# Two unused 96-byte tiles at the two ends of the SBUF partition, in a one-core fp32 attention and mixer block

## The chip, the core and the metric

The kernel runs on one core of one Trainium2 chip. TensorE (PE in the profile, its weight loads PEld) multiplies matrices, VectorE (DVE) and ScalarE (ACT) work on elements, GpSimd (POOL) does small jobs, and SyncE (SP) issues all transfers. The metric is the device time of one execution in microseconds. Operands of TensorE come from SBUF, 128 partitions wide; a matmul needs one operand that is loaded first (the weights, 128 columns here) and one that is streamed (the moving operand, 128 to 512 columns here). Results go to PSUM.

## The reference

For x of 2048 tokens by 576 columns, with xn the layernorm of x, the output is the sum of three things:

```python
q, k, v = split(xn @ wqkv)                       # 32 heads of 18
o = softmax(q . k[t - 2w], w = 0..7) @ v[t - 2w] # causal window of 8, dilation 2
A = o @ wo
h  = gelu(layernorm(xn) @ w1)                    # 576 x 576
hs = shift(h, [+1, -1, +2, -2] by column quarter) @ w2
x1 = xn + hs
B  = x1 + gelu(layernorm(x1) @ w3) @ w4          # 576 x 4608 x 576
out = x + A + B
```

All of it is fp32. The kernel reaches that accuracy on TensorE by splitting each operand into a rounded part (hi) and the remainder (lo), both as fp32r, and adding hi x hi, hi x lo and lo x hi.

## The kernel before, in words

The work on TensorE comes in stages, all written out in the order in which they run; nothing is planned at run time.

1. **QKV projection** (0 to about 196 us, lines L230 in `q_cg` and L133 in `mm_tok`). For each tile of 128 tokens the normalized tokens, transposed into `xt` by TensorE (L102, L105 in `transposes`; the identity is the moving operand), are the weights, and 288 or 432 columns of `WQ` move. Results are spilled to DRAM through the staging tile `stg`.
2. **First mixer matrix** (about 196 to 264 us, L380 and L395). Slices of `W1` are the weights, 512 tokens of `xt` move; the gelu goes into the eight `h` tiles.
3. **Second mixer matrix** (about 264 to 328 us, L133 again). Slices of the `h` tiles, shifted by one or two floats, are the weights; 288 columns of `W2` move.
4. **The MLP** (about 328 to 1250 us). `up` (L616) takes `W3` as weights and moves 512 columns of `xt` or `x1n`, 14 matmuls for one result. `down` (L636) takes slices of 128 columns of `hi` and `lo` as weights and moves 288 columns of `W4`; 12 matmuls make one result of 128 tokens, 48 make a block of 512. The attention on VectorE runs in between, in slices that a generator hands out (`bg`).
5. **The output projection** (about 1250 to 1318 us, L133 and L764): slices of `oT` as weights, 288 columns of `Wo` moving; then the rows of `Y` are stored.

SBUF is given out by pools that work as two stacks. Pools on the left grow upward from byte 40,608 of the partition, behind the fixed tiles of the pool `base`; pools with `side="right"` grow downward from byte 229,344. A pool that is closed gives its place to the next one on its side. Every tile begins at a multiple of 32 bytes. Tiles that matter to the change, with the byte at which they begin in the partition and that byte modulo 128:

| Tile | Side | Before | mod 128 | After | mod 128 |
|---|---|---|---|---|---|
| Y, ident (pool base) | left | 1152, 38016 | 0, 0 | the same | 0, 0 |
| WQ, W2 | left | 40608 | 32 | 40704 | 0 |
| h00 to h03 | left | 63648, 71872, 80096, 88320 | 32, 64, 96, 0 | each + 96 | 0, 32, 64, 96 |
| hi, lo | left | 45216 to 63648 | 32 | each + 96 | 0 |
| q, k, v, prod, o, L (attention) | left | 67744 and up | 32 (v 96) | each + 96 | 0 (v 64) |
| Wo, oT | left | 65696, 101536 and on | 32 | each + 96 | 0 |
| xin, first raw buffer | left | 109728, 116640 | 32 | each + 96 | 0 |
| second raw buffer, stg | left | 125280, 137952 and on | 96 | each + 96 | 64 |
| xt | right | 192480, 210912 | 96 | each - 96 | 0 |
| W1, W1R, z | right | 165344, 185824, 188384 | 96 | each - 96 | 0 |
| W3, W4, rawf | right | 163296, 178656, 153568 and on | 96 | each - 96 | 0 |
| x1n2, x1n3 | right | 116704, 135136 | 96 | each - 96 | 0 |

The slices that the matmuls take lie at multiples of 128 bytes from the start of their tile, but for three kinds: the 432-column slices of WQ (1728 bytes, so every second one is 64 further on), the slices of `h` (shifted by 4 or 8 bytes, behind two floats of margin) and T4 (8 bytes).

The lines of the prediction's steps:

```python
pe.matmul(ps[:, h, :n], xs(a), ws(b, h), ...)                                  # L133: weights, then moving
pe.matmul(ps, W3[f][:, w, :], x1n[b][:, a, :], ...)                            # L616
pe.matmul(ps[:, k, :HF], h[:, col], w[:, p, k * HF:(k + 1) * HF], ...)         # L636
```

Of the kernel before, what the change touches and what calls it, by code (L numbers as in the profile page):

```python
# [8 lines left out]
F32 = mybir.dt.float32  # L9
# [36 lines left out]
def fused_block(ctx, tc, x, wqkv, wo, w1, w2, w3, w4, out):  # L46
# [4 lines left out]

    ctx.enter_context(tc.manual_schedule())
    base = ctx.enter_context(tc.tile_pool(name="base", bufs=1))
    ring = ctx.enter_context(tc.tile_pool(name="ring", bufs=2, side="right", reuse_waits="tile"))
    psa = ctx.enter_context(tc.tile_pool(name="psa", bufs=2, space=PSUM))
    psb = ctx.enter_context(tc.tile_pool(name="psb", bufs=3, space=PSUM))
    dram = ctx.enter_context(tc.tile_pool(name="dram", bufs=1, space=DRAM))
# [738 lines left out]
```

## Time and profile before

| | |
|---|---|
| Median of 3 runs | 1322.92 us (1322.52 to 1323.04) |
| Profiled execution | 1322.94 us, span 1321.2 us |
| TensorE busy | 1312.1 us, 99% of the span |
| VectorE busy | 921.9 us, 70% |
| ScalarE busy | 348.2 us, 26% |
| Transfers | 93.76 MB, 23.9% of the 16 engines' time |

The page of the profile gives busy times by engine, slices of the span, the DMA queues, the chain of work that ended last, and the costliest groups of instructions. A row of a group reads: line, engine, operation, output tile <- input tiles, shapes, count | busy us, mean ns of one | idle us of the engine just before them, and what ended it. The time of one matmul in such a row is longer than the step from one matmul to the next, since matmuls overlap; the step is read from the chain, whose pieces are given as start, length, engine, tile, line and count. All groups of `W1`, `W2`, `W3` and `W4` stand under the name `W`.

### The profile page before, as it was taken

Reading aid. Unit: us, or ns where it says so; the run is one execution under the profiler, and the core shown is the slowest. Engines: PE = TensorE matmul, PEld = TensorE weight load, DVE = VectorE, ACT = ScalarE, POOL = GpSimd, SP = SyncE. Lnnn points to the kernel's source line nnn. Section 1 sums busy time; section 2 is a strip of 40 time slices with the busy share of each in tenths; the row PEclk is TensorE's granted clock in tenths of the full one; section 3 lists DMA queues with packets and bytes.
Section 4 is the critical chain, followed back from the end, with each engine's and each line's share of the span. In section 5 each row is a group of like instructions: output and inputs, shape, how many; then the busy total and the mean of one; then the engine's idle time right before and its main releaser. Section 6 shows DMA issues by size and latency. Waiting matters only on the chain.

```text
span 1321.2 us, 18855 instructions
## 1 busy us (share of the span) xinstructions
PE 1312.1 (99%) x7894; PEld 1208.0 (91%) x7894; DVE 921.9 (70%) x1332; ACT 348.2 (26%) x633; POOL 35.2 (3%) x92
## 2 busy tenths in 40 slices
PE   8999999999999999999999999999999999999998
PEld 8999998899899999999999999999999999999998
DVE  6443326687676778878868868878877886884454
ACT  4322225411423222222122222223213223122111
POOL 2010100011000000000000000000000000000000
PEclk9999999999999999999999999999999999999999
DMA  7644322020112021221221220220320200212164
GB/s 211 152 107 108 98 68 69 18 82 28 59 30 80 20 71 39 71 71 39 71 71 29 80 71 20 90 71 20 90 71 19 82 28 20 71 42 95 46 192 140
DMA packets 120325, 93.76 MB, mean 71 GB/s; under 512 B 73504, under 2 KB 100000, under 8 KB 120240
## 3 DMA queue, kind: packets, MB, share of 16 engines
q1 hardware_dynamic: 120240, 92.56, 23.9%
q8 instruction: 62, 1.02, 0.3%
q14 instruction: 23, 0.19, 0.0%
HBM read 67.83 MB, written 23.66 MB: 69 GB/s over the span
## 4 chain that ended last, share of the span: by engine, by line
PE 96%; DVE 2%; ACT 1%; SPq 1%; issue 1%; DMA 0%; POOL 0%; DVEq 0%; ACTq 0%; POOLq 0%
PE ps L636 34%; PE p L616 34%; PE ps L133 18%; PE ps L230 3%; PE p L380 3%; PE ps L102 2%; PE p L272 0%; PE p L395 0%; PE p L764 0%; DVE bn L88 0%; PE ps L105 0%; ACT xt L107 0%; DVE xt L111 0%; SPq L370 0%; DVE xt L114 0%
## 5 line engine op out<-in xcount | busy, mean ns | idle before, releaser
L636 PE MATMUL ps<-W,hi 128*128 128x288 f32 x2304 | 397.9, 294 | 0.5 <-DVE oT L114 0.5
L636 PEld LDWEIGHTS ps<-W,hi 128*128 128x128 f32 x2304 | 339.5, 188 | 6.1 <-PE ps L102 0.7
L620 ACT ACTIVATE hi<-p 128x512 fp32r<-128x512 f32 x144 | 86.2, 599 | 619.3 <-PE p L616 619.3
L636 PE MATMUL ps<-W,lo 128*128 128x288 f32 x1152 | 245.3, 294 | 0.0
L616 PE MATMUL p<-xt,W 128*128 128x512 f32 x1008 | 235.4, 390 | 0.0
L616 PE MATMUL p<-x1n,W 128*128 128x512 f32 x1008 | 234.9, 389 | 0.0
L622 DVE TENSOR_TENSOR lo<-g,hi 128x512 fp32r<-128x512 f32 x144 | 99.7, 692 | 193.2 <-ACT g L621 193.2
L639 DVE TENSOR_TENSOR Y<-ps,Y 128x576 f32<-128x576 f32 x288 | 212.8, 751 | 16.3 <-PE ps L636 16.1
L616 PEld LDWEIGHTS p<-x1n,W 128*128 128x128 f32 x1008 | 187.2, 188 | 36.8
L616 PEld LDWEIGHTS p<-xt,W 128*128 128x128 f32 x1008 | 187.1, 188 | 36.9
L636 PEld LDWEIGHTS ps<-W,lo 128*128 128x128 f32 x1152 | 185.4, 187 | 0.0
L133 PE MATMUL ps<-WQ,xt 128*128 128x432 f32 x672 | 135.3, 360 | 0.0
L133 PEld LDWEIGHTS ps<-WQ,xt 128*128 128x128 f32 x672 | 125.2, 188 | 5.2
L111 DVE TENSOR_TENSOR xt<-ps,xt 128x512 fp32r<-128x512 f32 x40 | 27.6, 689 | 87.2 <-ACT xt L110 52.1
L568 DVE TENSOR_TENSOR prod<-q,k 128x1152 f32<-128x1152 f32 x64 | 86.5, 1351 | 0.0
L571 DVE TENSOR_REDUCE L<-prod 128x64 f32<-128x1152 f32 x64 | 86.2, 1347 | 0.0
L621 ACT ACTIVATE g<-p 128x512 f32<-128x512 f32 x144 | 85.4, 593 | 0.0
L548 DVE TENSOR_TENSOR prod<-v,L 128x1152 f32<-128x1152 f32 x56 | 75.6, 1350 | 0.0
L552 DVE TENSOR_TENSOR o<-o,prod 128x1152 f32<-128x1152 f32 x56 | 75.6, 1350 | 0.0
L118 ACT CAST W<-rawf 128x640 fp32r<-128x640 f32 x72 | 50.5, 702 | 68.9 <-PE ps L636 62.2
L133 PE MATMUL ps<-Wo,oT 128*128 128x288 f32 x420 | 59.1, 298 | 0.2
L133 PEld LDWEIGHTS ps<-Wo,oT 128*128 128x128 f32 x420 | 56.2, 188 | 1.4 <-issue 1.4
(103 smaller groups left out, 941.9 us busy)
## 6 DMA issues: line engine op xcount, KB each, us to landing
qkvd<-stg SPq DMA_DIRECT2D x24, 432.0 KB, 3.4
rawf<-in_B_w_dram SPq DMA_DIRECT2D x36, 288.0 KB, 3.0
rawf<-in_B_w_dram SPq DMA_DIRECT2D x36, 256.0 KB, 2.9
xin<-in_A_x_dram SPq DMA_DIRECT2D x16, 288.0 KB, 3.8
q<-qkvd SPq DMA_DIRECT2D x8, 576.0 KB, 3.8
k<-qkvd SPq DMA_DIRECT2D x8, 576.0 KB, 5.7
v<-qkvd SPq DMA_DIRECT2D x8, 576.0 KB, 5.9
od<-o SPq DMA_DIRECT2D x8, 576.0 KB, 4.9
```

Source lines behind the costliest of these rows:

```text
L118: act.copy(dst_hi, raw)
L133: pe.matmul(ps[:, h, :n], xs(a), ws(b, h), start=i == 0, stop=i == len(PAIRS) - 1)
L548: dve.tensor_tensor(dst, vv, Lf[:, :, w:w + 1].to_broadcast([128, TPP * GH, HD]), op=ALU.mult)
L552: dve.tensor_tensor(o, o, dst, op=ALU.add)
L568: dve.tensor_tensor(prod.rearrange("p (j h) d -> p j (h d)", h=GH), q, k[:, r0:r0 + TPP, :], op=ALU.mult)
L571: dve.tensor_reduce(Lf[:, :, w], prod, axis=AX.X, op=ALU.add)
L616: pe.matmul(ps, W3[f][:, w, :], x1n[b][:, a, :], start=n == 0, stop=n == len(PAIRS) - 1)
L620: act.activation(hi, ps, AF.Gelu_apprx_tanh)
L621: act.activation(g32, ps, AF.Gelu_apprx_tanh)
L622: dve.tensor_tensor(lo, g32, hi.bitcast(F32), op=ALU.subtract)
L636: pe.matmul(ps[:, k, :HF], h[:, col], w[:, p, k * HF:(k + 1) * HF], start=n == 0, stop=n == len(seq) - 1)
L639: dve.tensor_tensor(yv, ps[:, :, :HF], yv, op=ALU.add)
```

## The change

Two pools are opened, each with one tile of 24 floats per partition that nothing uses: `edge` on the right ahead of the pool `ring`, and `lead` on the left behind the pool `base`. All later tiles on the right thereby lie 96 bytes lower and all later tiles on the left 96 bytes higher. The program's instructions, their order on each engine, their waits and their shapes are the same as before, apart from the addresses; four lines are added, so line numbers of the changed kernel are 4 higher.

```diff
     base = ctx.enter_context(tc.tile_pool(name="base", bufs=1))
+    edge = ctx.enter_context(tc.tile_pool(name="edge", bufs=1, side="right"))
+    edge.tile([128, 24], F32, name="lead_right")
     ring = ctx.enter_context(tc.tile_pool(name="ring", bufs=2, side="right", reuse_waits="tile"))
+    lead = ctx.enter_context(tc.tile_pool(name="lead", bufs=1))
+    lead.tile([128, 24], F32, name="lead_left")
     psa = ctx.enter_context(tc.tile_pool(name="psa", bufs=2, space=PSUM))
```

## The prediction

> **What bounds the kernel now.** I read the page first, for the engine that is never idle, then the chain of waits, because only work on it can move the end.
>
> ```profile
> span 1321.2 us, 18855 instructions
> PE 1312.1 (99%) x7894; PEld 1208.0 (91%) x7894; DVE 921.9 (70%) x1332; ACT 348.2 (26%) x633; POOL 35.2 (3%) x92
> PEclk9999999999999999999999999999999999999999
> q1 hardware_dynamic: 120240, 92.56, 23.9%
> PE 96%; DVE 2%; ACT 1%; SPq 1%; issue 1%; DMA 0%; POOL 0%; DVEq 0%; ACTq 0%; POOLq 0%
> ```
>
> TensorE is busy for 1312.1 of 1321.2 us at the full granted clock, and the chain runs through it for 96% of the span. VectorE (70%), ScalarE (26%) and the transfers (23.9% of the DMA engines) lie beside it. So a change of a few bytes in where tiles lie moves the end only if it changes how far apart two matmuls start. That distance is a group of the chain divided by its count.
>
> ```profile
> 18.27 25.44 PE ps L230 x168
> 43.71 0.44 PE ps L102 x4
> 98.79 10.98 PE ps L133 x56
> 173.04 0.44 PE ps L102 x4
> 303.40 0.44 PE ps L102 x4
> 308.41 3.70 PE ps L133 x28
> 312.66 3.71 PE ps L133 x28
> 316.81 3.73 PE ps L133 x28
> 390.85 6.36 PE p L616 x28
> 397.20 6.34 PE ps L636 x48
> 1254.11 0.44 PE ps L102 x4
> 1254.65 3.72 PE ps L133 x28
> 1258.84 3.95 PE ps L133 x28
> ```
>
> Each row is start, length and count. For 512 moving columns (L616) the step is 6360/28 = 227.1 ns; for 288 columns it is 6340/48 = 132.1 ns in L636, 132.1 to 133.2 ns in the three L133 groups at 308 to 317 us (W2 against h), 132.9 ns at 1254.65 us (Wo against oT); for 432 columns (WQ, 98.79 us) 10980/56 = 196.1 ns. Between 288 and 512 columns, 224 columns cost 95.0 ns, 0.424 ns a column; 132.1 - 288 x 0.424 = 10 ns is left as a fixed part of each matmul, whatever it is made of.
>
> **The change, part by part.** *New instructions: none.* Nothing reads or writes the two new tiles, and they cost 192 bytes of a partition. *Engines and transfers other than TensorE.* Their operands move by 96 bytes too. The trace of before has both kinds side by side:
>
> ```profile
> L639 DVE TENSOR_TENSOR Y<-ps,Y 128x576 f32<-128x576 f32 x288 | 212.8, 751 | 16.3 <-PE ps L636 16.1
> L119 DVE TENSOR_TENSOR W<-rawf,W 128x576 fp32r<-128x576 f32 x36 | 27.0, 749 | 0.0
> L622 DVE TENSOR_TENSOR lo<-g,hi 128x512 fp32r<-128x512 f32 x144 | 99.7, 692 | 193.2 <-ACT g L621 193.2
> L387 DVE TENSOR_TENSOR h<-g,h 128x512 fp32r<-128x512 f32 x16 | 11.1, 693 | 25.3 <-ACT g L386 25.1
> ```
>
> Y lies at a multiple of 128 bytes and takes 751 ns; rawf and W4 lie 96 past one and take 749 ns. lo lies at 32, and h is written 8 bytes past the starts of its tiles: 692 and 693 ns. Price 0, within 2 ns. What hides it anyway is that VectorE idles 30%; without that cover 1332 instructions by 2 ns would be 2.7 us. *First transfers and last store.* The head of the chain waits for no transfer:
>
> ```profile
> 1.37 5.38 PE p L272 x24
> 3.62 0.82 DVE L88 BATCH_NORM_STATS2 bn<-xin 128x6 f32<-128x288 f32 x2 [3.62 <-DMA xin<-in_A_x_dram]
> 6.67 0.77 ACT L118 CAST WQ<-raw 128x288 fp32r<-128x288 f32 x2 [4.65 <-DMA raw<-in_A_wqkv_dram]
> ```
>
> x lands at 3.62 us and the first weights at 6.67 us, while the 24 warm-up matmuls run to 6.75 us. Were their cover gone, a tenth off the 3.62 us would be 0.4 us either way. The last store reads Y, which does not move. Price 0.
>
> *Matmuls: how the two operands lie to each other.* TensorE reads the moving operand of one matmul while it loads the weights of the next. The trace shows that the distance between these two addresses matters. Four starts in a row in Wo against oT, each from a window so short that the row begins with that matmul:
>
> ```profile
> 1255.94 0.43 PE L133 MATMUL ps<-Wo,oT 128*128 128x288 f32 x2
> 1256.08 0.42 PE L133 MATMUL ps<-Wo,oT 128*128 128x288 f32 x2
> 1256.21 0.42 PE L133 MATMUL ps<-Wo,oT 128*128 128x288 f32 x2
> 1256.34 0.43 PE L133 MATMUL ps<-Wo,oT 128*128 128x288 f32 x2
> 1256.47 0.43 PE L133 MATMUL ps<-Wo,oT 128*128 128x288 f32 x2
> 1256.61 0.42 PE L133 MATMUL ps<-Wo,oT 128*128 128x288 f32 x2
> ```
>
> The steps are 0.14, 0.13, 0.13, 0.13, 0.14 us, and the long one comes every fourth time, when the moving slice lies 384 bytes past the weights, counted modulo 512 (slices of Wo are 1152 bytes apart, which is 128 modulo 512, so four slices go round). Call it 140 ns against 131.
>
> The Trainium skill (TensorE: Matmul & The Clock Gate, Step-by-step) says that TensorE reads the moving operand and the weights through two independent ports, so that loading the next weights takes nothing from the running matmul. The trace does not agree: 0.14 against 0.13 us by address alone. By that rule the next term would be nothing, and the sum 1322.9 us.
>
> Which distances change? L616 (W3 against xt and x1n) and L380 (W1 against xt) have both operands on the right side: both go down by 96, distance the same, 0. Wo against oT and W2 against h are both on the left: 0. WQ (left) against xt (right) changes by 192, but its slices of 1728 bytes go through all eight multiples of 64 modulo 512, before and after: 0. L636 alone changes its set: W4 (right) goes down by 96, hi and lo (left) up by 96, so its distances, 64, 192, 320 and 448 before, become 384, 0, 128 and 256, those of Wo against oT. In its six matmuls the order is 128, 256, 384, 0, 128, 256: one in six is at 384. By the short-window rows that is 131 + 9/6 = 132.5 ns against 132.1, +0.4 ns.
>
> ```profile
> L636 PE MATMUL ps<-W,hi 128*128 128x288 f32 x2304 | 397.9, 294 | 0.5 <-DVE oT L114 0.5
> L636 PE MATMUL ps<-W,lo 128*128 128x288 f32 x1152 | 245.3, 294 | 0.0
> L616 PE MATMUL p<-xt,W 128*128 128x512 f32 x1008 | 235.4, 390 | 0.0
> L616 PE MATMUL p<-x1n,W 128*128 128x512 f32 x1008 | 234.9, 389 | 0.0
> L133 PE MATMUL ps<-WQ,xt 128*128 128x432 f32 x672 | 135.3, 360 | 0.0
> L133 PE MATMUL ps<-Wo,oT 128*128 128x288 f32 x420 | 59.1, 298 | 0.2
> L133 PE MATMUL ps<-W,h 128*128 128x288 f32 x384 | 54.1, 296 | 0.0
> L380 PE MATMUL p<-xt,W 128*128 128x512 f32 x224 | 54.2, 395 | 0.8 <-ACT g L386 0.8
> ```
>
> L636 has 2304 + 1152 = 3456 matmuls: 0.4 ns each is +1.4 us. The upper end is the whole Wo group's 132.9 ns, +0.8 ns, +2.7 us; the lower end is that only the shares of slow and fast steps are dealt out anew, 0, since L636 and W2 against h have the same 132.1 ns at quite different distances. Half way, +0.7 us, is what I take: the groups with other distances lie between these ends.
>
> *Matmuls: where an operand starts by itself.* Before, every moving operand of a real matmul starts 32 bytes past a multiple of 64 (left side 32, right side 96 modulo 128, with slices that keep that). After, all start at a multiple of 64. No row of before shows such a matmul, so the price is bounded. For the weights, starts at 36, 76, 96 and 16 modulo 128 (the four h tiles, each shifted by one or two floats) give 132.1 to 133.2 ns a matmul, no worse than L636's 32. In the transposes the weights lie at 0 (Y, 43.71 us), 96 (z, 173.04), 32 or 64 (rz, 303.40) and 32 (ot, 1254.11): 0.44 us for four each time. For the moving operand only the transposes' identity lies at 0, at 440/4 = 110 ns for 128 fp32 columns, another form. The lower end is that the whole fixed 10 ns goes: over the 2304 + 1152 + 1008 + 1008 + 672 + 420 + 384 + 224 = 7172 matmuls shown, -72 us. The upper end, from the slow step of every fourth matmul, is +9 ns in a quarter of L636, 864 x 9 = +7.8 us. I take 0: of all rows the weights' are nearest, as they read the same SBUF by the same engine, and there a start that is off by even 4 bytes costs nothing.
>
> The Trainium skill (SBUF — State Buffer, Specifications) speaks against the change here: it gives SBUF lines of 16 bytes, and a tile at 32 or 96 already starts on one. By that rule this term is 0 as well; the weights' rows agree, and for moving operands no run here shows it yet.
>
> **Sum.** The profiled execution took 1322.94 us, 1.7 us more than its span and within 0.02 us of the median, 1322.92. With 0 + 0 + 0.7 + 0 the forecast is 1323.6 us: no change that can be told.
>
> **The rivals.** *A start off a 64-byte unit costs each matmul half a unit* (faster). Half of 64 bytes is 8 columns, 8 x 0.424 = 3.4 ns; over 7172 matmuls 24 us, so about 1299 us. For it: a fixed 10 ns that nothing in the trace explains, and the transposes, whose aligned identity needs 110 ns, little above 256 x 0.424 = 108.5 if a column takes two turns. Against it: the weights' indifference, and the 196.1 ns of WQ, whose fixed part is 196.1 - 432 x 0.424 = 13 ns at the same starts, so that it is not one constant of the start. If all the fixed part goes it is 1323 - 72 = 1251 us, which I hold for remote. *L636's new distances are worse than in Wo* (slower). If two of the six steps took 140 ns, the mean would be 131 + 3 = 134 ns: +1.9 x 3456 = +6.6 us, 1329.5 us. For it: the slow step exists, at a distance that L636 does not have now and gets. Against it: one in six, not two. It decides once a group of 48 takes over 6.38 us, as there are 72 groups and 0.2% is 2.65 us. *The change does not reach what counts* (no change): h01, h02 and h03 still lie at 32, 64 and 96, since each h tile takes 8224 bytes, and the staging and second raw buffers at 64; that costs nothing by the rows above, and gives 1322.9 us.
>
> **How the numbers follow.** A measurement of this kernel can hardly tell less than 0.2%, 2.65 us, from no change. No change holds 0.44, of which the sum above and the last rival are the same thing to within 0.7 us. Faster gets 0.30: the half unit and smaller relatives of it, from the gentler deal of distances to the remote full loss of the fixed part. Slower gets 0.26: the slow distance at two of six, or at one of six with 0.8 ns or more in all. The range goes from 1300, just above the half unit's 1299, to 1329, just short of two of six: beyond the ends I leave 0.1 below and 0.08 above. The likeliest case's own range is 1322 to 1326.
>
> **What would show it.** Right: L616's groups of 28 at 6.36 us and WQ's of 56 at 10.98 us, L636's of 48 between 6.34 and 6.38 us with one longer step in six, VectorE's four rows within 2 ns. Wrong: an L616 group below 6.30 us would show that the start itself counts, since its distances do not change; L636 above 6.38 us with L616 unchanged would show the distance; a chain that reaches its long run of L230, at 18.27 us before, over 0.4 us earlier or later would show transfers that I held for hidden.

## The result, and the profile after

The changed kernel takes 1328.02 us (median of 6 runs, 1327.91 to 1328.40) against 1322.82 us before on the same chip: ratio 1.0039, 95% interval 1.0027 to 1.0052. It is slower by 5.2 us, which is clear of the noise though only 0.4%. The forecast was 1323.6 us, no change; it gave this side a chance of 0.26. The time is inside the forecast's range of 1300 to 1329 us, close to its upper end. The page of the profile after:

```profile
span 1326.5 us, 18855 instructions
PE 1316.8 (99%) x7894; PEld 1211.7 (91%) x7894; DVE 921.9 (69%) x1332; ACT 347.9 (26%) x633; POOL 34.4 (3%) x92
PEclk9999999999999999999999999999999999999999
q1 hardware_dynamic: 120240, 92.56, 23.7%
```

The instructions, the clock and the transfers are the same, and VectorE's busy time is the same to 0.1 us; TensorE alone is busy longer. The chain of waits after (start, length, engine, tile, line, count; line numbers are 4 higher):

```profile
1.65 5.31 DMA raw<-in_A_wqkv_dram
18.38 25.43 PE ps L234 x168
98.89 11.02 PE ps L137 x56
304.43 3.72 PE ps L137 x28
308.90 3.72 PE ps L137 x28
313.16 3.72 PE ps L137 x28
404.16 6.37 PE p L620 x28
410.54 6.40 PE ps L640 x48
429.71 6.38 PE p L620 x28
1255.76 3.72 PE ps L137 x28
```

Down groups (L640) went from 6.34 to 6.40 us, that is from 132.1 to 133.3 ns a matmul; up groups (L620) from 6.36 to 6.37 or 6.38; WQ's 56 (98.89 us) from 10.98 to 11.02. W2 against h (304 to 313 us) and Wo against oT (1255.76) kept their 3.7 us, though every one of their operands moved by 96 bytes as well. The head ends 0.1 us later, at 18.38 instead of 18.27 us; it now runs through the first weights' transfer instead of the warm-up matmuls. Adding up the distances from each matmul's start to the next, after minus before, gives the whole account of the 5.38 us of span: the down matmuls +3.6, the up matmuls +1.3, WQ's L137 +0.4, the head and the rest +0.1; W2, Wo and L384 are each within 0.1 us.

Nine starts in a row in the down matmuls of the changed kernel, again from windows so short that the row begins with that matmul:

```profile
615.31 0.43 PE L640 MATMUL ps<-W,lo 128*128 128x288 f32 x2
615.45 0.29 PE L640 MATMUL ps<-W,lo 128*128 128x288 f32 x1
615.58 0.43 PE L640 MATMUL ps<-W,hi 128*128 128x288 f32 x2
615.71 0.43 PE L640 MATMUL ps<-W,hi 128*128 128x288 f32 x2
615.84 0.43 PE L640 MATMUL ps<-W,hi 128*128 128x288 f32 x2
615.98 0.29 PE L640 MATMUL ps<-W,hi 128*128 128x288 f32 x1
616.11 0.43 PE L640 MATMUL ps<-W,lo 128*128 128x288 f32 x2
616.24 0.29 PE L640 MATMUL ps<-W,lo 128*128 128x288 f32 x1
616.37 0.43 PE L640 MATMUL ps<-W,hi 128*128 128x288 f32 x2
```

The steps are 0.14, 0.13, 0.13, 0.13, 0.14, 0.13, 0.13, 0.13: the long step of Wo against oT has come to the down matmuls, and it comes with every fourth one. Over all 288 down results, the steps 0, 4 and 8 of the twelve take 141.5, 139.7 and 139.8 ns, the others 130.8 to 131.6.

VectorE's four rows of the prediction:

```profile
L643 DVE TENSOR_TENSOR Y<-ps,Y 128x576 f32<-128x576 f32 x288 | 212.5, 749 | 16.9 <-PE ps L640 16.4
L626 DVE TENSOR_TENSOR lo<-g,hi 128x512 fp32r<-128x512 f32 x144 | 99.6, 692 | 197.5 <-ACT g L625 197.5
L123 DVE TENSOR_TENSOR W<-rawf,W 128x576 fp32r<-128x576 f32 x36 | 26.9, 747 | 0.0
L391 DVE TENSOR_TENSOR h<-g,h 128x512 fp32r<-128x512 f32 x16 | 11.1, 692 | 25.3 <-ACT g L390 25.1
```

All four are within 2 ns of before: 749 for 751, 747 for 749, 692 for 692, 692 for 693.

### The profile page after: what moved, and what is told of

Read it like the earlier page. It is cut to its first block, busy times and chain, and to the rows that moved or that the text cites. A ratio compares the mean times of both kernels' runs of the same rounds, so it can differ in the third digit from the quotient of the medians.

```text
span 1326.5 us, 18855 instructions
## 1 busy us (share of the span) xinstructions
PE 1316.8 (99%) x7894; PEld 1211.7 (91%) x7894; DVE 921.9 (69%) x1332; ACT 347.9 (26%) x633; POOL 34.4 (3%) x92
## 4 chain that ended last, share of the span: by engine, by line
PE 95%; DVE 2%; ACT 1%; SPq 1%; issue 1%; DMA 1%; DVEq 0%; ACTq 0%
PE ps L640 35%; PE p L620 34%; PE ps L137 18%; PE ps L234 3%; PE p L384 2%; PE ps L106 2%; DMA raw<-in_A_wqkv_dram 0%; PE p L399 0%; PE p L768 0%; DVE xt L115 0%; ACT xt L111 0%; PE ps L109 0%; SPq L374 0%; DVE xt L118 0%; DVE bn L92 0%
## 5 line engine op out<-in xcount | busy, mean ns | idle before, releaser
L640 PE MATMUL ps<-W,hi 128*128 128x288 f32 x2304 | 401.6, 296 | 0.5 <-DVE oT L118 0.5
L640 PEld LDWEIGHTS ps<-W,hi 128*128 128x128 f32 x2304 | 342.5, 189 | 6.5 <-PE ps L106 0.7
L640 PE MATMUL ps<-W,lo 128*128 128x288 f32 x1152 | 247.5, 296 | 0.0
L620 PE MATMUL p<-xt,W 128*128 128x512 f32 x1008 | 236.0, 390 | 0.0
L620 PE MATMUL p<-x1n,W 128*128 128x512 f32 x1008 | 235.7, 390 | 0.0
L620 PEld LDWEIGHTS p<-x1n,W 128*128 128x128 f32 x1008 | 187.1, 188 | 37.2
L620 PEld LDWEIGHTS p<-xt,W 128*128 128x128 f32 x1008 | 187.0, 188 | 37.2
L640 PEld LDWEIGHTS ps<-W,lo 128*128 128x128 f32 x1152 | 185.2, 189 | 0.0
L137 PE MATMUL ps<-WQ,xt 128*128 128x432 f32 x672 | 135.7, 361 | 0.0
L137 PEld LDWEIGHTS ps<-WQ,xt 128*128 128x128 f32 x672 | 125.4, 188 | 5.4
L137 PE MATMUL ps<-Wo,oT 128*128 128x288 f32 x420 | 59.1, 298 | 0.2
L137 PEld LDWEIGHTS ps<-Wo,oT 128*128 128x128 f32 x420 | 56.3, 188 | 1.4 <-issue 1.4
```

The lines of the kernel that those rows point to most:

```text
L137: pe.matmul(ps[:, h, :n], xs(a), ws(b, h), start=i == 0, stop=i == len(PAIRS) - 1)
L620: pe.matmul(ps, W3[f][:, w, :], x1n[b][:, a, :], start=n == 0, stop=n == len(PAIRS) - 1)
```

## The experiments

In what follows "distance" is the address of a matmul's moving operand minus that of the weights, modulo 256 bytes; the third run below shows that 256 is enough for the down matmuls, and the runs on the up distance show it for the up matmuls. The weights' slices of neighbouring matmuls are equal modulo 256 in the up and down groups, so these runs cannot tell the matmul's own weights from the next one's.

### Which bytes count: four paddings

The theory of the distance says that what slows the down matmuls is where W4 lies against hi and lo. It has two rivals: a start at a multiple of 128 bytes is slow by itself, or the tiles of the other engines disturb TensorE from there.

Both paddings 32 bytes:

```diff
-    edge.tile([128, 24], F32, name="lead_right")
+    edge.tile([128, 8], F32, name="lead_right")
-    lead.tile([128, 24], F32, name="lead_left")
+    lead.tile([128, 8], F32, name="lead_left")
```

> Both paddings are 32 bytes instead of 96, so every tile lies at 64 modulo 128 and none at a multiple of 128; the distance between W4 and hi or lo in the down matmuls changes by 64 bytes, again to multiples of 128. Theory of the distance (a down matmul is slower when its moving operand and the next weights lie a multiple of 128 bytes apart): 1328.0 us, down groups of 48 at 6.39 to 6.40 us, as with the 96 bytes. Rival theory of the start (an operand that starts at a multiple of 128 bytes is slower by itself): 1322.8 us, groups at 6.34. Rival theory of the neighbours (tiles of the other engines at multiples of 128 bytes disturb TensorE): 1322.8 us.

Measured: 1326.92 us (1326.72 to 1327.36) against 1322.96, ratio 1.0030 (1.0019 to 1.0042).

```profile
404.09 6.37 PE p L620 x28
410.46 6.38 PE ps L640 x48
```

No operand of the up and down matmuls lies at a multiple of 128 now, and most of the loss is there: the start is out as its cause. Other than expected, v, `stg`, the second raw buffer and h02 do come to multiples of 128 here (they lay at 96), so the neighbours are put out only by the third run. The down groups are at 6.38, not 6.39 to 6.40; the same three long steps are at 138.0, 137.3 and 139.7 ns, and they sit one matmul later in the group.

96 bytes on the left and 32 on the right:

```diff
-    edge.tile([128, 24], F32, name="lead_right")
+    edge.tile([128, 8], F32, name="lead_right")
```

> 96 bytes on the left, 32 on the right: left tiles lie at multiples of 128 as in the changed kernel, right tiles at 64 modulo 128; the distance of the down matmuls changes by 128, so it stays at odd multiples of 64 as before. Distance: 1322.8 us, down groups of 48 at 6.34 us and up groups of 14 without the 9 ns that the changed kernel adds to each. Start: hi, lo, WQ, W2, Wo and oT still start at multiples of 128, so between 1325 and 1328 us. Neighbours: the attention's tiles lie as in the changed kernel, so 1328 us.

Measured: 1325.08 us (1324.82 to 1325.73), ratio 1.0017 (1.0008 to 1.0026).

```profile
410.15 6.34 PE ps L640 x48
416.49 6.39 PE p L620 x28
```

The down groups are back at 6.34 us with hi, lo, WQ, W2, Wo and oT still at multiples of 128, as the distance has it. The forecast of 1322.8 failed at the up groups: 6.39 instead of 6.36. The distance within them is what it was; their middle steps are at 226.7 ns as in all these runs, but of the 28 matmuls behind a down group the first eight step unevenly, by 224 to 236 ns, where before only the first two were longer (232.3 and 230.8 ns).

64 bytes ahead of hi and lo in the changed kernel, and 64 behind them:

```diff
+    shift = ctx.enter_context(tc.tile_pool(name="shift", bufs=1))
+    shift.tile([128, 16], F32, name="hp_shift")
     hp = ctx.enter_context(tc.tile_pool(name="hp", bufs=2, reuse_waits="tile"))
+    even = ctx.enter_context(tc.tile_pool(name="even", bufs=1))
+    even.tile([128, 16], F32, name="ap_shift")
     apc = tc.tile_pool(name="ap", bufs=1, reuse_waits="tile")
```

> The changed kernel with 64 bytes more ahead of hi and lo alone, and 64 more behind them, so that the attention's tiles and Wo and oT still lie at multiples of 128. Distance: the down matmuls are back at odd multiples of 64, 48 of them at 6.34 us; 3.6 us return from them and 1.3 us from the up groups if their 9 ns come from the down matmuls ahead of them; 1323 us, or 1324.3 if the up groups keep theirs. Start: W4, W3, xt and x1n still start at multiples of 128, so at most half comes back, 1325 to 1328 us. Neighbours: 1328 us.

Measured: 1323.15 us (1322.98 to 1323.61), ratio 1.0002 (0.9993 to 1.0011).

```profile
409.99 6.34 PE ps L645 x48
416.33 6.36 PE p L625 x28
```

Moving the tiles of the down matmuls' weights by 64 bytes gives back 4.9 of the 5.2 us, the up groups' share with it, while W4, W3, xt and x1n stay where they were, and Wo, oT and the attention's tiles, 128 bytes further on, keep their places modulo 128. This settles the cause of the loss. Against the kernel before, the distance of the down matmuls differs here by exactly 256 bytes, and each of the twelve steps agrees with before to 0.1 ns: 256 bytes is a period. It also shows that the longer steps of the up groups are brought along by the down groups beside them.

The padding on the left alone:

```diff
-    edge = ctx.enter_context(tc.tile_pool(name="edge", bufs=1, side="right"))
-    edge.tile([128, 24], F32, name="lead_right")
```

> The padding on the left alone: the distance of the down matmuls changes by 96 bytes, to odd multiples of 32, a class that no run has shown; the same for WQ against xt. Distance: somewhere from 1322 to 1328 us, and only L640, the WQ groups and the first matmuls of the up groups differ from before; the W2, Wo and up steps in the middle of a group stay at their times. Start: left operands at multiples of 128, 1325 to 1328 us, with W2 and Wo groups slower too. Neighbours: 1328 us.

Measured: 1329.73 us (1329.47 to 1330.05), ratio 1.0052 (1.0040 to 1.0065).

```profile
404.90 6.39 PE p L618 x28
411.29 6.39 PE ps L638 x48
```

Half the padding costs more than all of it: +6.8 us. The down matmuls, at distances 96 and 224 in turn, take 133.1 ns (6.39/48), +3.4 us in all; the ends of the up groups cost 2.6 us, twice as much as in the changed kernel. W2 and Wo groups kept their steps to 0.1 us in sum, as the distance has it and the start has not.

### The distance of the up matmuls

It was 0 in every run so far, before and after. From the kernel before, W3 and W4 were moved by 64, 128, 192 and 32 bytes; x1n2, x1n3, hi and lo follow so that, of all distances modulo 256, that of the up matmuls alone changes; xt stays, and the tiles behind hi and lo move along together. For 64:

```diff
+    wsh = ctx.enter_context(tc.tile_pool(name="wsh", bufs=1, side="right"))      # ahead of wp
+    wsh.tile([128, 16], F32, name="w_shift")
+    xsh = ctx.enter_context(tc.tile_pool(name="xsh", bufs=1, side="right"))      # ahead of xp
+    xsh.tile([128, 48], F32, name="x_shift")
+    shift = ctx.enter_context(tc.tile_pool(name="shift", bufs=1))                # ahead of hp
+    shift.tile([128, 48], F32, name="hp_shift")
```

> From the kernel before: W3 and W4 64 bytes lower, x1n2 and x1n3 256 lower in all, hi and lo 192 higher. So the distance of the down matmuls stays (modulo 256), and that of the up matmuls, 0 in every run so far, becomes 64. If up matmuls gain from leaving the multiples of 128 as the down matmuls lose by coming to them (about 1 ns each), 2016 of them give 2 us: 1321 us, an up group of 28 at 6.33 us. If 512 columns are long enough to make the distance indifferent, the middle of a group stays at 226.7 ns and the time at 1323 us, give or take the settling steps at the head of a group.

> The same with 128 bytes: the up distance becomes 128, the down distance stays. Theory that the class modulo 128 decides: middle of an up group 226.7 ns as before. The order of the first steps of a group may shift; 1323 to 1325 us.

> The same with 192 bytes: the up distance becomes 192, in the class of 64. Middle of an up group as with 64 bytes; the head of the group is in another phase. 1321 to 1325 us.

> The same with 32 bytes: the up distance becomes 32, an odd multiple of 32, the class in which the down matmuls took longest (133.3 ns and more with the padding on the left alone). If the class acts alike on 512 columns, up steps are over 1 ns longer, +2 us, 1325 us; if 512 columns are indifferent, 1323 us.

| Up distance | Time, us | Ratio (interval) | Up steps in the middle of a group, ns |
|---|---|---|---|
| 0 (before) | 1322.88 | 1 | 226.7 |
| 64 | 1331.23 | 1.0063 (1.0047 to 1.0080) | 233.3, or 231.7, 225.8 and 229.2 in turn (see below) |
| 128 | 1335.42 | 1.0095 (1.0082 to 1.0108) | 237.5 and 229.2 in turn, mean 233.3 |
| 192 | 1335.37 | 1.0094 (1.0080 to 1.0109) | 233.3 |
| 32 | 1335.94 | 1.0098 (1.0085 to 1.0111) | 233.3, 234.2, 230.8 and 235.0 in turn, mean 233.3 |

Up and down groups from the chains of the four kernels, 64, 128, 192 and 32 in this order:

```profile
410.14 6.34 PE ps L642 x48
416.48 6.43 PE p L622 x28
467.57 6.43 PE p L622 x28
480.44 6.53 PE p L622 x28
```

```profile
404.09 6.53 PE p L622 x28
410.62 6.35 PE ps L642 x48
```

```profile
403.96 6.54 PE p L622 x28
410.49 6.34 PE ps L642 x48
```

```profile
404.12 6.54 PE p L622 x28
410.66 6.35 PE ps L642 x48
```

Every one of the four expectations fell. I had asked whether distance 0 costs the up matmuls 1 ns, and it is the best of the five places: at 32, 128 and 192 the 2016 matmuls take 6.6 ns more each, and the time is 12 to 13 us longer. The patterns differ, but the mean of 233.3 ns is the same. At 128 the operands of the up matmuls begin at the same places modulo 128 as before, so it is not the start that counts here either. For the blocks in xt the distance is 32, 128 or 192, for those in x1n 256 less, and their steps agree to 0.2 ns: 256 bytes is a period at 512 columns too. The down groups stayed at 6.34 or 6.35 us. The runs at 64 fall into two groups, 1328.1 to 1328.6 and 1333.9 to 1334.8 us; the profile is of the second. In it the 8 up groups of 28 up to the one at 467.57 us take 6.43 us (229.6 ns a step), the one ahead of them and all from 480.44 us on take 6.53 (233.2 ns); 72 groups at 0.07 us more than before would be +5 us and at 0.17 us +12 us, which is close to the two times; the faster executions themselves were not profiled. So there are two ways to run through the same addresses, and what moves the engine from one to the other stays open. This also shows what the changed kernel was spared: both operands of the up matmuls are on the right side, so the padding left their distance at 0.

### Two tries to gain from it

Projection at distance 0 throughout, 448 and 416 columns instead of 432 twice:

```diff
-        mm_tok(ps, lhs(t), lambda b, i: WQ[:, b, (2 * h + i) * CG:(2 * h + i + 1) * CG], CG)
+        xs, c = lhs(t), wq(2 * h * CG)     # wq: columns from 864 on lie 32 columns further on
+        for i, (a, b) in enumerate(PAIRS):
+            ends = dict(start=i == 0, stop=i == len(PAIRS) - 1)
+            pe.matmul(ps[:, 0, 64:512], xs(a), WQ[:, b, c:c + 448], **ends)
+            pe.matmul(ps[:, 1, 0:416], xs(a), WQ[:, b, c + 448:c + 864], **ends)
```

> From the kernel before: in the projection the 864 columns of a half are split 448 and 416 instead of 432 and 432, the second half of WQ begins 128 bytes further on, and WQ lies 64 bytes higher, so that every moving slice of L133 lies at distance 0 modulo 256 from its weights in xt. If distance 0 costs a fixed 32 columns' time, as in the up groups (226.7 ns for 512), the pair takes 200 + 187 = 387 ns instead of 392, and 336 pairs give 1.6 us: 1321.3 us. If the distance is indifferent here, 1322.9 us with the pair at 392 ns.

> The same, and oT 64 bytes higher against Wo, which puts the output projection into the class that the down matmuls have (132.2 instead of 133.0 ns): another 0.3 us off, 1321.0 us. If the distance is indifferent there, as g_wq.

Measured: 1323.24 us, ratio 1.0003 (0.9994 to 1.0012), and with oT moved as well 1323.30 us, 1.0003 (0.9994 to 1.0012). In the chain of the first, two starts 27 pairs apart (L246 is the first matmul of a pair):

```profile
98.89 0.21 PE ps L246
109.51 0.20 PE ps L246
```

The pair takes 10620/27 = 393.3 ns, where 391.8 was measured before (10.97 us for 28 pairs) and 387 expected, so distance 0 does not cost the same fixed time at every width. Wo's groups gave 0.2 us in the trace, less than a measurement tells.

Down matmuls at distance 0 throughout, 320 and 256 columns instead of 288 twice:

```diff
-            for k in range(2):
-                pe.matmul(ps[:, k, :HF], h[:, col], w[:, p, k * HF:(k + 1) * HF],
-                          start=n == 0, stop=n == len(seq) - 1)
+            ends = dict(start=n == 0, stop=n == len(seq) - 1)
+            pe.matmul(ps[:, 0, 192:512], h[:, col], w[:, p, 0:320], **ends)
+            pe.matmul(ps[:, 1, 0:256], h[:, col], w[:, p, 320:576], **ends)
```

> From the kernel before: the down matmuls split 576 columns as 320 and 256 instead of 288 and 288, so that all slices of W4 lie at multiples of 256 bytes from its start, and hi and lo lie 64 bytes higher: distance 0 modulo 256 for every down matmul. If distance 0 costs 32 columns' time each, the pair takes 147 + 120 = 267 ns against 264.4 before: +4 us, 1327 us. If distance 0 is the best there is for any width, as it is for 512 columns, the pair falls below 264 ns and the time below 1323 us.

Measured: 1327.65 us (1327.50 to 1328.00), ratio 1.0036 (1.0022 to 1.0050). In the chain, the first of these starts and the one eleven pairs on:

```profile
437.01 0.15 PE ps L638
439.94 0.15 PE ps L638
```

That is 2930/11 = 266 ns a pair against 264.4, close to the first of the two answers (267), though not in its parts: over all down results the 320 columns take 149 ns and the 256 take 117.5, not 147 and 120. The down matmuls cost 3.3 us and the ends of the up groups 1.3. So distance 0 is not enough to make a step short: 512 columns do best there among the five distances tried, but 320 and 256 columns there are slower than 288 twice with 64 and 192 in turn, which is what the kernel before has. Whether 320 and 256 would do better at another distance was not run. No kernel of these runs beats the kernel before.

## Why the prediction was right or wrong, point by point

- *TensorE's step from matmul to matmul is the only thing that counts.* Right. All but 0.1 of the 5.38 us of span are in it, and VectorE's rows moved by 2 ns at most.
- *First transfers and last store: 0.* Right in size, 0.1 us. But the head's chain does run through the first weights' transfer after the change; it and the warm-up matmuls were level.
- *Where an operand starts by itself: 0.* Right, and shown: W2 and Wo groups moved by 96 bytes with unchanged distance and kept their steps, up groups keep 226.7 ns in the middle at multiples of 128 (after) and at 64 modulo 128 (both paddings 32). The rival of half a 64-byte unit is out. The Trainium skill gives SBUF lines of 16 bytes (SBUF — State Buffer, Specifications), and by that a start at 32 or 96 is no worse than one at 0. These moving operands agree, with the same 226.7 ns at 96, 0 and 64 modulo 128.
- *L616 distance unchanged: 0.* Wrong by 1.3 us. The step in the middle of an up group is unchanged as said, but each group of 14 pays about 9 ns more on average, in the first four steps behind a down group (236.6, 228.5, 232.4 and 230.8 ns for 232.3, 230.8, 226.8 and 226.5) and in the step into the next one (232.5 for 225.7). The prediction assumed that a matmul's time hangs on its own distance alone; the run with 64 bytes ahead of hi and lo shows that what the down groups beside it do counts too.
- *WQ against xt: the same eight distances, 0.* Wrong by 0.4 us. The set is the same, but within each half of the columns two distances alternate, and these pairs are others now. That does not explain it all: with 96 bytes on the left and 32 on the right the pairs are those of before, with the halves exchanged, and the L137 steps add up to 133.3 us as in the changed kernel, against 132.9 before. What makes the 0.4 us stays open.
- *L636 gets the distances of Wo against oT.* The mechanism was right: this set of distances is slower, and giving back the distance gives back the time. The size was wrong, and it is this term that failed: +0.7 us forecast, 0 to 2.7 us as its bounds, +3.6 us measured. The reading that the long step belongs to one distance, 384 modulo 512, was false. In the six rows that it rests on, every fourth matmul has that distance, so the count and the distance could not be told apart; in the down matmuls one in six has it, but one in four is long. Counting by fours gives 131 + 9/4 = 133.25 ns against the measured 133.3. The rest of the same Wo group could have told: its fourth and eighth matmul lie at 384 as well, and their steps are short. Here are the starts of the fourth and fifth matmul and of the eighth and ninth.

```profile
1254.89 0.43 PE L133 MATMUL ps<-Wo,oT 128*128 128x288 f32 x2
1255.02 0.43 PE L133 MATMUL ps<-Wo,oT 128*128 128x288 f32 x2
1255.42 0.55 PE L133 MATMUL ps<-Wo,oT 128*128 128x288 f32 x3
1255.55 0.42 PE L133 MATMUL ps<-Wo,oT 128*128 128x288 f32 x2
```

  Both steps are 0.13 us. The mean of a Wo group, 132.9 ns, was too low a bound for the same reason, since long steps come only from its twelfth matmul on. In the traces, wherever the distances are 0 and 128 in turn (Wo against oT before and after, the down matmuls with both paddings at 96 and at 32), the long step, once it has set in, is every second one of those at 128; why every second, no run shows.
- *The rival of two in six.* It came true in kind, with one in four instead; it named 6.38 us as the length of a group of 48 from which it decides, and the group is at 6.40. It is this rival that set the upper end of the range at 1329 us. The likeliest case's own range, 1322 to 1326 us, misses the 1328.0 measured, so that the range holds the time is owed to the width left for the rivals, and not to the sum.

The Trainium skill states that weights load through a port of their own and take nothing from the running matmul (TensorE: Matmul & The Clock Gate, Step-by-step). The prediction set this aside on the false reading above; the runs give better ground for doubt, since moving nothing but addresses takes an up step from 226.7 to 233.3 ns. They show that the step hangs on the distance between the two operands, and not whether it is the loading that costs.

## What to carry to other kernels

When TensorE is the bound, compare steps from start to start of matmuls, by operand pair, before and after any change in where tiles lie: a pool that is opened, padded or made larger on one side shifts that side's operands against the other side's, with no change in the program. Aligning tiles to a round number bought nothing here; what counted was the distance between moving operand and weights modulo 256 bytes, and the best one is to be measured for each width and order of slices. A pattern read from a stretch in which two explanations coincide (one distance, every fourth matmul) should be priced by both, and held against every other step of the group that has one without the other.

## What the runs showed of the hardware that I had not expected

- Up matmuls of 512 columns took 226.7 ns at distance 0 and 233.3 ns on average at 32, 128 and 192, 12 to 13 us over the kernel by 32 to 192 bytes of address. At 64 they took either 233.3 or 228.9 ns on average.
- Step times follow the distance with a period of 256 bytes. What the group ahead does is felt for up to eight matmuls: with 96 and 32 bytes of padding an up group's first eight steps are 224 to 236 ns, and 226.7 after them, at an unchanged distance.
- At the same addresses up groups can run in either of two lengths, 6.43 and 6.53 us, and change over within an execution. Why, and what in the SBUF or TensorE makes the period, no run here shows; whether a matmul's own weights or the next one's count was not tried.
